# Two attentions with a gate on one Trainium2 core: parity order of the sequence, x^T phi(k) instead of v, a hand-set TensorE order, crossbar-transposed output of B

## The chip, the cores and the metric

One core of one Trainium2 chip runs the whole program. The metric is device time of one execution in microseconds (us). The kernel before was run beside every changed kernel on the same chip; its median lies between 567.8 and 569.9 us from session to session. A ratio below is the mean time of one kernel's fast runs over that of the kernel before in the same rounds, with a 95% interval, so it is not quite the ratio of the medians quoted beside it.

Names: PE is TensorE, PEld its weight loads, DVE VectorE, ACT ScalarE, POOL GpSimd, SP the engine whose queue issues most DMAs. "Matmul" without a size means 128x512 bf16 with 128 rows of contraction. Scores are q . k of B, PV is the product of the softmax weights with V, and a chunk is four heads of B. `Ob` is what PV gives, by rows; `OBT` is its transpose, which the output product needs. The crossbar is what a transposing DMA goes through. The kv stretch runs from the last matmul of v (later of x^T phi(k)) to the first of V.

## The reference, cut to what matters

```python
# x = A_x: (1, 2048, 1024) bf16; H = 32 heads of Dh = 32; wqkv: (1024, 3072); wo: (1024, 1024)
g = sigmoid((x * gate_w).sum(-1, keepdims=True))
# A: linear attention
phi = lambda t: where(t > 0, t + 1, exp(t)) + 1e-6
kv  = einsum("bhsd,bhse->bhde", phi(k), v)          # per head, 32x32, over all positions
z   = sum over s of phi(k)
a   = (phi(q) kv) / (phi(q) . z + 1e-6)  @ A_wo
# B: each position sees 8 keys, at distance 0, 2, 4, ..., 14
b   = softmax(q . k[s - 2*w] * Dh**-0.5, w = 0..7) v[s - 2*w]  @ B_wo
out = g * a + (1 - g) * b
```

Two facts carry the change. A query of B only ever sees keys of its own parity. And kv = phi(k)^T v = phi(k)^T x Wv, so it can be had as (x^T phi(k))^T Wv, without v.

## The kernel before

It keeps x^T in SBUF (`xT`, 8 blocks of 128 x 2048) and has three stages. Cuts are marked.

```python
# stage 1: k of A, v of A, kv, Wo products
nc.sync.dma_start_transpose(out=xT[:, :, 0:128], in_=x[0:128, :])
WkA = load_w("WkA", A_wqkv, D)                       # 2 MB, same queue
for s0, s1_ in ((128, 512), (512, 1024), (1024, S)):
    nc.sync.dma_start_transpose(out=xT[:, :, s0:s1_], in_=x[s0:s1_, :])
# ... pk = phi(x WkA): 256 matmuls; vA = x WvA: 256 matmuls ...
for c in range(KT):
    kvp = ps_kv.tile([P, P + 1], F32, name="kvp", tag="kv")
    for t in range(NB):
        nc.tensor.matmul(kvp[:], lhsT=pk[:, t, c * P:(c + 1) * P], rhs=vA[:, t, c, :], ...)
    # ... mask to the diagonal blocks (DVE), transpose on PE, copy (ACT) into KVT ...
# ... W2 = KVT^T WoA: 16 matmuls, copies alternating between ACT and DVE ...

# stage 2: B. 18 tiles of 113 queries (the first 127) with 128 keys each; V is projected once per tile
for c in range(KT):                                  # 4 heads at a time
    # ... kT, qT of these heads: 64 matmuls ...
    for g, tiles in enumerate(GROUPS):               # 6 groups of 3 tiles
        # 12 scores (32 rows each) -> exp on ACT -> mask on DVE -> 12 PV matmuls
        # -> reciprocal and scale on DVE -> Ob
        for tt, (q0, w, k0) in enumerate(tiles):
            nc.tensor.transpose(out=tr[:, tt, 0:w], in_=Ob[0:w, tt]..., identity=ident[0:w, 0:w])
        for w, ts in parts:
            nc.scalar.copy(out=OBT[:, c, ...], in_=tr[:, ts, 0:w])

# stage 3, for each quarter of the rows: q of A, phi, denominator, then both output products
for b in range(4):
    for c in range(KT):
        # 8 matmuls pjq -> phi -> pq
        nc.tensor.matmul(den[:], lhsT=Zb[:, c, :], rhs=pq[:], start=True, stop=True)
        # ln, exp on ACT; pqs = pq * that on DVE
    # ... 4 x 2 x (8 matmuls OBT x WoB, 8 matmuls pqs x W2), combine, store ...
```

The order on each engine is not written here: a scheduler in the kernel framework places the instructions, from the order in which the program is written and its own estimate of times.

The softmax here doesn't subtract the row's maximum and nothing guards it: scores larger than these inputs give would overflow.

## Time and profile before

| | before |
|---|---|
| time, median (lowest to highest) | 568.17 us (567.44 to 569.76), 3 runs |
| PE busy | 530.1 us, 93% |
| DVE, ACT busy | 252.7 us (44%), 232.9 us (41%) |
| matmuls of 128x512 | 2128 |

Lines of the page's first two parts for the kernel before: busy time, share and instruction count of an engine; then busy tenths of PE and the granted TensorE clock in 40 slices of the span.

```profile
...
PE 530.1 (93%) x3495; PEld 242.9 (43%) x3560; DVE 252.7 (44%) x469; ACT 232.9 (41%) x372; POOL 15.5 (3%) x62
...
PE   2999999996999999999999999969999999999997
...
PEclk9999999999799999999999999988999999999999
...
```

PE is the bound, but a busy PE is no measure of how full it is. Count instead: steady matmuls start 0.216 us apart (the skill, "TensorE: Matmul & The Clock Gate", section "Back-to-back issue gap", gives N/2.4 + 2.5 ns for an isolated matmul on a warm array; the trace agrees with that, and not with the shorter pace that the section gives for real kernels). 2128 of them are 460 us. The other 108 us are what a change can still take. PE in each stretch of the kernel before, cut at the boundaries that the chain of waits shows (stretch, its length, busy time and instructions, granted clock, DMA share, GB/s):

```profile
...
core 0: us, PE busy (x), PEclk, DMA share, GB/s
0.00:14.10 14.10, 3.57 (x8) 1.00 0.92 236
...
125.70:146.50 20.80, 13.61 (x151) 0.92 0.00 1
...
224.50:368.00 143.50, 138.61 (x1562) 1.00 0.03 9
368.00:382.30 14.30, 9.76 (x161) 0.87 0.00 1
382.30:564.90 182.60, 176.70 (x783) 0.98 0.07 23
...
```

125.7 to 146.5 holds 16 matmuls of 128x512 and 128 of 128x129: it is the kv sums and the Wo products. 224.5 to 368 is seven chunks of B's attention, 20.5 us each, of which 64 projection matmuls are 13.8. 368 to 382.3 is the last chunk, with PE busy 9.8 of 14.3 us.

A piece of one such chunk, PE instructions in order of time (start, length, line, shapes, count; in brackets idle time before and what ended it):

```profile
...
230.47 0.27 PE L243 MATMUL s_1929<-qT,kT 32*128 32x113 bf16 x6
230.81 0.32 PE L270 MATMUL tr<-ident,Ob 113*128 113x113 bf16 x3
231.06 0.28 PE L243 MATMUL s_1929<-qT,kT 32*128 32x113 bf16 x6
231.27 0.60 PE L230 MATMUL pjkq<-xT,WkB_86 128*128 128x512 bf16 x2
231.71 0.46 PE L257 MATMUL oB<-V,PT_1362 128*128 128x33 bf16 x12
232.02 0.81 PE L230 MATMUL pjkq<-xT,WkB_86 128*128 128x512 bf16 x3
...
```

The scheduler cuts the 12 scores in two and puts three transposes between (0.25 us to the start of what follows). PE is never idle for long, but 1.1 us of each group's 3.4 us is not projection (20.5 and 13.8 us over six groups).

### The profile page before, as it was taken

What the parts mean: (1) busy time and instruction counts of PE and PEld (TensorE: products, weight loads), DVE (VectorE), ACT (ScalarE), POOL (GpSimd) and SP (SyncE); (2) the same over time, 40 slices, a digit from 0 to 9 for tenths busy, and PEclk for the clock granted to TensorE, in tenths of its full rate; (3) what the DMA queues carried; (4) which work ended last, traced back from release to release, by engine and by line L of the source; (5) the groups of instructions that cost most, each with busy time, mean ns of one, the idle gap of its engine ahead of it and who ended that gap; (6) DMA issues with size and microseconds to landing.
All of it is one profiled execution on the core that took longest, in us unless ns stands there. A gap on an engine that the chain in (4) does not pass through costs nothing.

```text
span 568.5 us, 8370 instructions
## 1 busy us (share of the span) xinstructions
PE 530.1 (93%) x3495; PEld 242.9 (43%) x3560; DVE 252.7 (44%) x469; ACT 232.9 (41%) x372; POOL 15.5 (3%) x62
## 2 busy tenths in 40 slices
PE   2999999996999999999999999969999999999997
PEld 0444444444344444444444444433344344344343
DVE  1467971003311112755665575575524534533542
ACT  1233333333211112665575575565514623622631
POOL 9100000000000000000000000000000000000000
PEclk9999999999799999999999999988999999999999
DMA  9997460200202011000020000000010010010011
GB/s 236 280 349 246 119 195 4 71 1 1 74 1 74 1 30 45 2 3 1 1 75 1 2 1 2 2 2 0 19 39 17 1 56 20 0 48 28 1 37 38
DMA packets 40246, 30.17 MB, mean 53 GB/s; under 512 B 17552, under 2 KB 38032, under 8 KB 40208
## 3 DMA queue, kind: packets, MB, share of 16 engines
q1 hardware_dynamic: 40208, 29.63, 17.4%
q8 instruction: 28, 0.46, 0.3%
q14 instruction: 10, 0.08, 0.1%
HBM read 21.23 MB, written 4.19 MB: 45 GB/s over the span
## 4 chain that ended last, share of the span: by engine, by line
PE 68%; DVE 16%; ACT 8%; DMA 3%; issue 3%; SPq 1%; DVEq 0%; ACTq 0%
PE pj L129 14%; PE pjkq L230 14%; PE pjv L210 11%; PE pa L326 8%; PE pb L320 7%; DVE pq L305 3%; ACT ld L310 3%; PE pjq L298 3%; PE oB L257 3%; DVE Ob L265 2%; PE den L308 2%; PE tr L270 2%; ACT PT_1362 L249 2%; DMA xT<-in_A_x_dram 2%; DVE gjunk L153 2%
## 5 line engine op out<-in xcount | busy, mean ns | idle before, releaser
L129 PEld LDWEIGHTS <-xT 128*128 128x128 bf16 x512 | 50.6, 99 | 74.6 <-issue 9.2
L328 DVE SCALAR_TENSOR_TENSOR osb<-pa,gall,ob 128x512 bf16<-128x512 f32 x32 | 23.7, 750 | 56.7 <-PE pa L326 52.3
L323 ACT ACTIVATE ob<-pb,omgall 128x512 f32<-128x512 f32 x32 | 22.0, 687 | 60.5 <-PE pb L320 52.5
L210 PEld LDWEIGHTS <-xT 128*128 128x128 bf16 x288 | 28.5, 99 | 36.7 <-issue 2.2
L235 DVE CAST qT<-pjkq 128x512 bf16<-128x512 f32 x32 | 22.0, 688 | 42.4 <-PE pjkq L230 39.6
L129 PE MATMUL pj<-WkA_67,xT 128*128 128x512 bf16 x126 | 30.9, 407 | 10.7 <-DMA WkA_67<-in_A_wqkv_dram 8.0
L138 ACT ACTIVATE e<-pj 128x512 f32<-128x512 f32 x32 | 19.1, 597 | 51.5 <-PE pj L129 38.5
L320 PEld LDWEIGHTS <-OBT 128*128 128x128 bf16 x256 | 25.2, 98 | 29.7 <-issue 0.8
L310 ACT ACTIVATE ld<-den,eps 128x512 f32<-128x512 f32 x32 | 22.0, 687 | 35.7 <-PE den L308 35.7
L218 DVE CAST V<-pjv 128x512 bf16<-128x512 f32 x18 | 12.5, 694 | 52.3 <-PE pjv L210 52.3
L233 ACT CAST kT<-pjkq 128x512 bf16<-128x512 f32 x32 | 18.7, 586 | 37.7 <-PE pjkq L230 37.7
L320 PE MATMUL pb<-WoB_1336,OBT 128*128 128x512 bf16 x128 | 34.0, 385 | 0.0
L210 PE MATMUL pjv<-WvB_82,xT 128*128 128x512 bf16 x141 | 32.6, 392 | 1.1 <-DVE W_1311 L187 0.8
L230 PE MATMUL pjkq<-xT,WkB_88 128*128 128x512 bf16 x116 | 32.3, 380 | 0.8 <-issue 0.6
L230 PE MATMUL pjkq<-xT,WqB_695 128*128 128x512 bf16 x124 | 32.6, 379 | 0.3
L230 PE MATMUL pjkq<-xT,WkB_86 128*128 128x512 bf16 x119 | 31.8, 379 | 0.7 <-issue 0.5
L298 PE MATMUL pjq<-xT,WqA_1729 128*128 128x512 bf16 x122 | 31.3, 394 | 1.1 <-DVE qT L235 0.6
L147 ACT CAST vA<-pj 128x512 bf16<-128x512 f32 x32 | 18.8, 587 | 33.0 <-PE pj L129 31.9
L216 ACT CAST V<-pjv 128x512 bf16<-128x512 f32 x18 | 10.6, 588 | 52.9 <-PE pjv L210 50.1
L230 PE MATMUL pjkq<-xT,WqB_693 128*128 128x512 bf16 x124 | 31.8, 379 | 0.2
L320 PE MATMUL pb<-WoB_1338,OBT 128*128 128x512 bf16 x120 | 31.8, 379 | 0.2
L210 PE MATMUL pjv<-WvB_84,xT 128*128 128x512 bf16 x141 | 31.1, 379 | 0.2
(267 smaller groups left out, 771.4 us busy)
## 6 DMA issues: line engine op xcount, KB each, us to landing
xt<-in_A_x_dram SPq DMA_DIRECT2D x16, 256.0 KB, 2.6
out_dram<-osb SPq DMA_DIRECT2D x32, 128.0 KB, 1.7
WkA_67<-in_A_wqkv_dram SPq DMA_DIRECT2D x1, 1024.0 KB, 5.8
WkA_69<-in_A_wqkv_dram SPq DMA_DIRECT2D x1, 1024.0 KB, 8.2
WvA_74<-in_A_wqkv_dram SPq DMA_DIRECT2D x1, 1024.0 KB, 5.5
WvA_76<-in_A_wqkv_dram SPq DMA_DIRECT2D x1, 1024.0 KB, 7.8
WoA_78<-in_A_wo_dram SPq DMA_DIRECT2D x1, 1024.0 KB, 11.6
WoA_80<-in_A_wo_dram SPq DMA_DIRECT2D x1, 1024.0 KB, 13.3
```

What stands on the lines that cost most here:

```text
L129: nc.tensor.matmul(pj[:], lhsT=xT[:, kt, t * P:(t + 1) * P], rhs=W[half][:, kt, :], start=(kt == 0), stop=(kt == KT - 1))
L138: nc.scalar.activation(out=e[:], in_=pj[:], func=ACT.Exp)
L147: nc.scalar.copy(out=vA[:, t, half * 4:(half + 1) * 4, 0:P], in_=pj[:].rearrange("p (c e) -> p c e", c=4))
L210: nc.tensor.matmul(pj[:], lhsT=xT[:, kt, k0:k0 + P], rhs=WvB[half][:, kt, :], start=(kt == 0), stop=(kt == KT - 1))
L230: nc.tensor.matmul(pj[:], lhsT=W[c // 4][:, kt, (c % 4) * P:(c % 4 + 1) * P], rhs=xT[:, kt, cols], start=(kt == 0), stop=(kt == KT - 1))
L235: nc.vector.tensor_copy(out=dst[:, cols], in_=pj[:])
L298: nc.tensor.matmul(pj[:], lhsT=WqA[c // 4][:, kt, (c % 4) * P:(c % 4 + 1) * P], rhs=xT[:, kt, cols], start=(kt == 0), stop=(kt == KT - 1))
L310: nc.scalar.activation(out=ld[:], in_=den[:], func=ACT.Ln, bias=eps[:])
L320: nc.tensor.matmul(pb[:], lhsT=OBT[:, c, tb * P:(tb + 1) * P], rhs=WoB[half][:, c, :], start=(c == 0), stop=(c == KT - 1))
L323: nc.scalar.activation(out=ob[:], in_=pb[:], func=ACT.Copy, scale=omgall[:, tb:tb + 1])
L326: nc.tensor.matmul(pa[:], lhsT=pqs[:, c, t * P:(t + 1) * P], rhs=W2[half][:, c, :], start=(c == 0), stop=(c == KT - 1))
L328: nc.vector.scalar_tensor_tensor(out=osb[:, ncols], in0=pa[:], scalar=gall[:, tb:tb + 1], in1=ob[:], op0=ALU.mult, op1=ALU.add)
```

## The change

Its intent: fewer matmuls, no PE transposes, no stretch in which PE waits.

- **Parity order.** x is read, and the result written, even rows first, then odd. Keys of a query are then 8 neighbours, tiles are 112 queries (128 for the first of each parity), V of B is projected on 16 tiles and shifted copies are made by DMAs inside SBUF: 32 matmuls fewer.
- **x^T phi(k).** 256 matmuls in place of the 256 of v, then 64 of 128x128 with Wv in place of 128 of 128x129. z comes from 15 adds of 128x1024 on DVE and eight small fp32 products. No kv transposes.
- **Crossbar.** Ob goes to OBT by a transposing DMA. That needs 112 or 128 partitions; 113 and 127 do not fit (the skill, "DMA: Bandwidth & Descriptors", section "DMA Transpose (X-bar)", asks for a multiple of 16).
- **Order.** All of PE is under a fixed order, the order of writing. Scores and PV of chunk c are written among the projections of chunk c+1, Wo products among those of V, denominators among the output products.

The core of the diff (long; cut):

```diff
-    nc.sync.dma_start_transpose(out=xT[:, :, 0:128], in_=x[0:128, :])
-    WkA = load_w("WkA", A_wqkv, D)
-    for s0, s1_ in ((128, 512), (512, 1024), (1024, S)):
-        nc.sync.dma_start_transpose(out=xT[:, :, s0:s1_], in_=x[s0:s1_, :])
+    WkA = load_w("WkA", A_wqkv, D, eng=nc.scalar, parts=2)
+    for s0, s1_ in ((0, 128), (128, 256), (256, 512), (512, 1024), (1024, 1536), (1536, S)):
+        nc.sync.dma_start_transpose(out=xT[:, :, s0:s1_], in_=rows(x, s0, s1_))
 ...
+    with tc.manual_schedule(engines={PE}):
 ...
+            for half in range(2):
+                for kt in range(KT):
+                    pj = ps_1.tile([P, 512], F32, name="g_ps", tag="p1")
+                    for t in range(NB):
+                        nc.tensor.matmul(pj[:], lhsT=xrow[:, t, kt * P:(kt + 1) * P],
+                                         rhs=pk[:, t, half * 512:(half + 1) * 512], ...)
+                    nc.scalar.copy(out=g_[:, kt, :], in_=pj[:])
+            # zacc: 15 adds over t; gate: 16 reductions
+            for half in range(2):
+                kvp = ps_1.tile([P, 4, P], F32, name="kv_ps", tag="p1")     # one bank
+                for i in range(4):
+                    for kt in range(KT):
+                        nc.tensor.matmul(kvp[:, i, :], lhsT=WvA[half][...], rhs=G[half][...], ...)
+                    nc.vector.tensor_tensor(out=KVT[:, half * 4 + i, :], in0=kvp[:, i, :], in1=bdmask[:], ...)
 ...
-                    nc.tensor.transpose(out=tr[:, tt, 0:w], in_=Ob[0:w, tt]..., identity=ident[0:w, 0:w])
-                    nc.scalar.copy(out=OBT[:, c, ...], in_=tr[:, ts, 0:w])
+                        nc.sync.dma_start_transpose(
+                            out=OBT[:, c, q0:q0 + m * w].rearrange("p (t s) -> p t s", t=m),
+                            in_=Ob[0:w, t0:t0 + m].rearrange("p t i e -> p (t i e)"))
 ...
+                for g in range(len(GROUPS)):          # 5 groups, of 4, 4, 4, 3, 3 tiles
+                    ev.append((3 + 12.8 * g, lambda g=g: scores(g)))
+                    ev.append((3 + 12.8 * g + 17, lambda g=g: pv(g)))
 ...
+                interleave(list(kq_units(c, kqt)), [e for e in ev if e[0] < 64])   # ev: chunk c-1
```

## The prediction

> **What bounds it now.** TensorE. The page's first part gives PE 530.1 of 568.5 us (93%); VectorE is at 44%, ScalarE at 41%. The chain of waits shows eight 128x512 matmuls in 1.73 us, 0.216 us each; the Trainium skill, "TensorE: Matmul & The Clock Gate", section "Back-to-back issue gap", states N/2.4 + 2.5 ns, so the trace agrees and these matmuls cannot be made faster, only fewer or closer together. There are 2128 of them: 460 us. The other 108 us, by stretches of the chain:
> - 0 to 14.1: steady work starts only when the second transposed piece of x has landed; only 8 matmuls before it. About 12.4 us lost.
> - 125.7 to 146.5: kv sums, transposes and the product with Wo, PE waiting on VectorE and ScalarE; granted clock 0.78 at the end. 16 useful big matmuls in 20.8 us: about 17 lost.
> - 224.7 to 368: seven periods of 20.5 us, of which 64 projections are 13.8; the rest is scores, PV, transposes (three take about 0.26 us, six groups a period) and turns between them.
> - 368 to 382.3: the last chunk's attention with little to fill it, PE busy 9.8 of 14.3.
> - 382.3 to 564.9: four blocks of 45.65 us holding 200 big matmuls (43.3).
>
> **What the change does.** Big matmuls 2128 -> 2096 (V on 16 tiles, not 18): -7 us. V projection of A (256) becomes x^T phi(k) (256): equal. 128 kv matmuls of 129 columns become 64 of 128; the 8+144 TensorE transposes go; Wo products move into the V stage. Attention goes among the next chunk's projections in a fixed order, and its tail among the query projection of A. 128/112-row tiles suit the crossbar: the skill, "DMA: Bandwidth & Descriptors", section "DMA Transpose (X-bar)", wants a multiple of 16 partitions; no run yet shows a transfer that breaks this. Before, a crossbar transpose held the queue 0.17 us per 128x128 block (20.3 us for 120); 18 blocks in 8 transfers a period are then some 3 us plus fixed cost, off the critical path.
>
> Added VectorE work in the first stage: 16 adds of 128x1024 for z (estimate 1.2 us each from the 1.22 us gate reduction), which the order puts, with 10 gate reductions, among the 32 phi(k) (1.12 us each). That is about 62 us against 55.4 of TensorE, and the first reduction waits for x rows queued behind all transposes (about 26 us). Six PSUM banks absorb most; I expect a PE stall of about 5 us there.
>
> **Sum (us).** Start 9; k projection 55.4 + stall 5; x^T phi(k) 55.5; kv and z 7.5; V with Wo products 59; first k/q chunk 14; seven periods of 19.0 = 133 (13.8 + scores 2.7 + PV 1.9 + turns and small stalls; no transposes); query block with last attention 20.5; remaining 736 big matmuls 159.5 + 2; end 3.5. Total 524.
>
> **Prediction: 524 us, 512 to 538.** Faster by over 2%: 0.97; within 2%: 0.025; slower: 0.005.
>
> **What would show each step.** PE busy about 97%; steady matmuls from 9 us or less; idle PE before k-projection matmuls released by VectorE phi(k), some 5 us in total between 25 and 70 us; about 7 us between the last x^T phi(k) and first V matmul, clock near 1; a period of 18.5 to 19.5 us; PE idle under 1 us in the query block; output blocks without waits on pq or ld.
>
> **What would make it wrong.** SBUF-to-SBUF transposes slower than those from HBM: then Ob (two buffers) holds VectorE, and PV and projections follow (period over 20). Two projection banks with in-order ScalarE and VectorE (VectorE some 14.5 us of each 19) stalling PE. Fp32 z matmuls costing more than 0.3 us each. VectorE not holding up the first stage (then 518).

## The result

| | before, same rounds | after |
|---|---|---|
| time, median (lowest to highest) | 567.81 us (567.31 to 569.76) | 518.45 us (516.1 to 519.9), 4 runs |
| ratio | | 0.9121 (0.908 to 0.9162) |
| PE busy | 530.1 us, 93% | 494.4 us, 96% |
| DVE busy | 252.7 us | 262.6 us |
| ACT busy | 232.9 us | 209.4 us |

The same lines of the page for the changed kernel:

```profile
...
PE 494.4 (96%) x3328; PEld 230.2 (45%) x3328; DVE 262.6 (51%) x553; ACT 209.4 (40%) x323; POOL 8.1 (2%) x27
...
PE   2899999999899999999999999989999999999996
...
PEclk9899999999999999999999999999999999999999
...
```

PE by stretch in the changed kernel, cut at its own stages (first matmuls, k projection, x^T phi(k), kv and z, V with Wo products, first k/q chunk, seven chunks with attention, query block with the last attention, the rest, the end):

```profile
...
core 0: us, PE busy (x), PEclk, DMA share, GB/s
0.00:15.40 15.40, 3.41 (x8) 1.00 0.94 201
15.40:72.75 57.35, 56.34 (x249) 0.97 0.88 262
72.75:128.00 55.25, 55.25 (x260) 1.00 0.06 20
128.00:136.56 8.56, 6.27 (x82) 1.00 0.42 137
136.56:195.29 58.73, 58.73 (x274) 1.00 0.32 94
195.29:209.70 14.41, 14.41 (x72) 1.00 0.52 168
209.70:333.90 124.20, 123.13 (x1445) 1.00 0.22 47
333.90:354.40 20.50, 18.00 (x219) 1.00 0.15 28
354.40:513.50 159.10, 158.84 (x736) 1.00 0.08 27
...
```

256 matmuls of x^T phi(k) take 55.25 us, 0.2158 us each: nothing is left there. The last stage, from 354.4, holds 736 big matmuls in 159.1 us, again 0.216 each; in the kernel before each quarter there lost some 2.4 us (45.65 us for 200 matmuls). The gain by stage: kv 20.8 to 8.6 us, with 3.5 us of Wo products moved; a chunk 20.5 to 17.6; the end of attention and stage 3 together 196.9 (from 368 to 564.9) to 179.6 (from 333.9 to 513.5).

PE in one chunk of the changed kernel, in order of time, to be laid beside the same view of before:

```profile
...
227.30 1.25 PE L266 MATMUL kq_ps<-xT,WkB_101 128*128 128x512 bf16 x5
228.39 0.46 PE L315 MATMUL oB<-V,PT_1008 128*128 128x33 bf16 x12
228.69 1.89 PE L266 MATMUL kq_ps<-xT,WqB_568 128*128 128x512 bf16 x8
230.51 0.38 PE L292 MATMUL s_1826<-kqt 32*128 32x112 bf16 x16
230.82 1.04 PE L266 MATMUL kq_ps<-xT,WkB_101 128*128 128x512 bf16 x4
...
```

Sixteen scores of 32 rows go in 0.31 us, 16 PV matmuls in 0.41 us (12 in 0.30), uncut, and no transposes: 12.8 projections fit between two groups.

One thing went backwards. PE's first lines:

```profile
...
9.55 3.41 PE L153 MATMUL pk_ps<-WkA_72,xT 128*128 128x512 bf16 x8 [9.55 <-DMA xT<-in_A_x_dram]
15.44 20.85 PE L153 MATMUL pk_ps<-WkA_72,xT 128*128 128x512 bf16 x88 [2.47 <-DMA xT<-in_A_x_dram]
36.70 1.89 PE L153 MATMUL pk_ps<-WkA_72,xT 128*128 128x512 bf16 x8 [0.41 <-DVE pk L140]
38.78 1.89 PE L153 MATMUL pk_ps<-WkA_72,xT 128*128 128x512 bf16 x8 [0.19 <-DVE pk L140]
...
```

Steady matmuls start at 15.4 us, later than before (14.1), and not at 9 as predicted. The lines of 36.7 and 38.8 are the stall behind DVE that was forecast at 5 us; it is 0.8 us in all, in three waits. Another 1.9 us went in the 88 matmuls before it: they took 20.9 us, at a granted clock of 0.92.

### The profile page after: what moved, and what is told of

Read it like the earlier page. It is cut to its first block, busy times and chain, and to the rows that moved or that the text cites. A ratio compares the mean times of both kernels' runs of the same rounds, so it can differ in the third digit from the quotient of the medians.

```text
span 517.1 us, 8148 instructions
## 1 busy us (share of the span) xinstructions
PE 494.4 (96%) x3328; PEld 230.2 (45%) x3328; DVE 262.6 (51%) x553; ACT 209.4 (40%) x323; POOL 8.1 (2%) x27
## 4 chain that ended last, share of the span: by engine, by line
PE 82%; DVE 9%; SPq 5%; DMA 3%; issue 1%; ACT 0%; DVEq 0%
PE d_ps L410 21%; PE kq_ps L266 21%; PE v_ps L237 11%; PE g_ps L165 11%; PE d_ps L362 8%; SPq L96 5%; PE oB L315 3%; DVE pk L140 2%; DVE gjunk L179 2%; DMA OBT<-Ob 2%; DVE e L139 1%; PE q_ps L362 1%; PE den L395 1%; DMA xrow<-in_A_x_dram 1%; PE pk_ps L153 1%; PE kv_ps L191 1%
## 5 line engine op out<-in xcount | busy, mean ns | idle before, releaser
L165 PE MATMUL g_ps<-pk,xrow 128*128 128x512 bf16 x256 | 55.4, 379 | 0.0
L153 PEld LDWEIGHTS <-xT 128*128 128x128 bf16 x256 | 25.6, 101 | 46.7 <-DMA xT<-in_A_x_dram 12.7
L153 PE MATMUL pk_ps<-WkA_72,xT 128*128 128x512 bf16 x128 | 31.7, 409 | 12.8 <-DMA xT<-in_A_x_dram 12.0
L139 DVE TENSOR_SCALAR e<-e 128x512 f32<-128x512 f32 x64 | 26.6, 421 | 32.1 <-ACT e L138 32.1
L165 PEld LDWEIGHTS <-xrow 128*128 128x128 bf16 x256 | 25.0, 98 | 30.2
L237 PEld LDWEIGHTS <-xT 128*128 128x128 bf16 x256 | 25.1, 98 | 30.0
L324 DVE TENSOR_TENSOR Ob<-oB,rd 128x256 bf16<-128x256 f32 x80 | 31.4, 393 | 3.8 <-DMA OBT<-Ob 2.6
L266 PE MATMUL kq_ps<-xT,WkB_103 128*128 128x512 bf16 x128 | 32.9, 380 | 0.0
L266 PE MATMUL kq_ps<-xT,WqB_570 128*128 128x512 bf16 x128 | 32.9, 379 | 0.0
L266 PE MATMUL kq_ps<-xT,WkB_101 128*128 128x512 bf16 x128 | 32.3, 379 | 0.0
L266 PE MATMUL kq_ps<-xT,WqB_568 128*128 128x512 bf16 x128 | 32.2, 379 | 0.0
L410 PE MATMUL d_ps<-WoA_93,pqs 128*128 128x512 bf16 x128 | 31.7, 379 | 0.0
L410 PE MATMUL d_ps<-WoB_3861,OBT 128*128 128x512 bf16 x128 | 31.2, 379 | 0.0
L410 PE MATMUL d_ps<-WoB_3859,OBT 128*128 128x512 bf16 x128 | 30.7, 379 | 0.0
L410 PE MATMUL d_ps<-WoA_95,pqs 128*128 128x512 bf16 x128 | 30.7, 379 | 0.0
L237 PE MATMUL v_ps<-WvB_99,xT 128*128 128x512 bf16 x128 | 30.6, 379 | 0.0
## 6 DMA issues: line engine op xcount, KB each, us to landing
WvA_89<-in_A_wqkv_dram SPq DMA_DIRECT2D x1, 1024.0 KB, 15.4
```

What stands on the lines that cost most here:

```text
L139: nc.vector.tensor_scalar(out=e[:], in0=e[:], scalar1=1.0, scalar2=1e-6, op0=ALU.min, op1=ALU.add)
L153: nc.tensor.matmul(pj[:], lhsT=xT[:, kt, t * P:(t + 1) * P], rhs=WkA[half][:, kt, :], start=(kt == 0), stop=(kt == KT - 1))
L165: nc.tensor.matmul(pj[:], lhsT=xrow[:, t, kt * P:(kt + 1) * P], rhs=pk[:, t, half * 512:(half + 1) * 512], start=(t == 0), stop=(t == NB - 1))
L237: nc.tensor.matmul(st["pj"][:], lhsT=xT[:, kt, t * P:(t + 1) * P], rhs=WvB[half][:, kt, :], start=(kt == 0), stop=(kt == KT - 1))
L266: nc.tensor.matmul(st["pj"][:], lhsT=W[c // 4][:, kt, (c % 4) * P:(c % 4 + 1) * P], rhs=xT[:, kt, cols], start=(kt == 0), stop=(kt == KT - 1))
L324: nc.vector.tensor_tensor(out=Ob[:, 2 * b:2 * b + m], in0=oBv[:, b, 0:m, :, 0:Dh], in1=rd[:, b, 0:m].broadcast_to([P, m, 4, Dh]), op=ALU.mult)
```

## The experiments

Twelve runs, in three sessions: 1 to 4 on one chip, 6 to 9 on one, and 5 with 10 to 12 on one.

**1. Is it the hand-set order?** The changed kernel without it:

```diff
-    with tc.manual_schedule(engines={PE}):
+    with ExitStack():
```

> The changed kernel, written in the same interleaved order, but the TensorE order is left to the scheduler. Theory A (the hand-set order is what gains in the attention stage): 535 us or more, the period of a chunk back near 20 us. Theory B (the order in which the program is written already carries most of it, the scheduler keeps it): 516 to 526 us, period 17.6 to 18.5 us. I lean to B.

Measured: 512.91 us (512.6 to 513.36), ratio 0.9004 (0.898 to 0.9028). Faster than the changed kernel; neither theory had that. Theory A falls: a chunk takes 17.6 us here too. The order that gains is the one in which the program is written, and the scheduler keeps it. Where the fixed order loses, the trace shows. PE in the kv stretch, first the changed kernel:

```profile
...
127.84 0.61 PE L191 MATMUL kv_ps<-G_572,WvA_89 128*128 128x128 bf16 x8
128.83 0.61 PE L191 MATMUL kv_ps<-G_572,WvA_89 128*128 128x128 bf16 x8 [0.38 <-DVE KVT L194]
129.82 0.61 PE L191 MATMUL kv_ps<-G_572,WvA_89 128*128 128x128 bf16 x8 [0.38 <-DVE KVT L194]
...
```

and the same stretch under the scheduler:

```profile
...
127.67 4.02 PE L191 MATMUL kv_ps<-G,WvA 128*128 128x128 bf16 x64
131.53 1.90 PE L198 MATMUL z_ps<-ones,zacc 128*128 128x1 f32 x16
...
```

The four groups of `kv_ps` share one PSUM bank, and the framework lets PE write to a bank only after DVE has read what stands in it (the skill, "PSUM — Partial Sum Buffer", section "PSUM bank collisions raise a hardware error", says that two engines on one bank at once are an error; no run here made one, they show only the wait). In the fixed order PE stands 0.38 us at each of six groups. Under the scheduler DVE reads one group every 0.44 to 0.55 us while PE goes on with the next without a wait. So neighbouring groups must lie in different banks, which means that the scheduler takes the two halves in turn; the trace doesn't name the banks. (Run 9, which keeps the fixed order and only moves the reads, loses the wait too.) From the first kv matmul to the first of V the scheduler's kernel takes 5.6 us in place of 8.6. The rest of its 6 us (of the two spans, 517.1 and 511.1) is at a late crossbar transfer (below) and at the last PV, where the fixed order lets PE stand 1.2 us behind Ob while matmuls of the next block are ready.

**2. Is it the interleaved writing?** Attention written after its own chunk's projections, as before, order left to the scheduler:

```diff
             for c in range(KT):
                 kqt = kq.tile([P, 2, S], BF16, name="kqt", tag="kq")
-                ev = carry + (attention_events(c - 1, prev) if c else [])
-                interleave(list(kq_units(c, kqt)), [e for e in ev if e[0] < 64])
-                carry = [(p - 64, f) for p, f in ev if p >= 64]
+                interleave(list(kq_units(c, kqt)), [])
+                for p_, f in sorted(attention_events(c, kqt), key=lambda e: e[0]):
+                    f()
 ... (and the same at the query projection: nothing is interleaved there)
```

> The changed kernel with attention written after its own chunk's projections as in the kernel before, and TensorE order left to the scheduler. If order and interleaving are what gains, the period returns to the 20.5 us of before less about 1.6 us of TensorE transposes, some 19 us, and the last attention shows again as a stretch with PE idle (about 4 us): 532 to 542 us. Rival (the gain of the stage comes from having no transposes and fewer, larger groups): 522 us or less.

Measured: 525.24 us (524.9 to 526.7), ratio 0.9228 (0.9196 to 0.9261). The period is 19.0 us as expected (two periods in 38.1, the next two in 37.7), but the total fell between the two theories, since it was set against 518 us, while the fair partner is run 1 with 512.9. Against that, writing attention among the next projections is worth 12.3 us. Nearly all of it falls before the query block: both kernels start their first k/q matmul at 192.0 us, and the last one starts at 340.3 us here, at 328.7 in run 1. That is some 1.3 to 1.4 us in each of seven periods, and one wait of 1.8 us at 224.8. The last attention costs next to nothing: PE is idle there for 1.3 us in four waits, not the 4 us expected, since the scheduler fills it with the query projection.

**3. What does any interleaving hide?** The same writing, PE held to it:

> Attention written after its own chunk and TensorE held to exactly that order, so nothing fills the wait for exponentials. Scores wait for one set of four banks: about 2.5 us for each of five groups plus a tail, some 11 us of extra time in each of eight chunks: 590 to 620 us, with PE idle before scores released by ScalarE. If it is under 560 the wait behind the exponentials is not what interleaving hides.

Measured: 610.13 us (609.73 to 611.1), ratio 1.0712 (1.0682 to 1.0743): the time is in the range, the account of it only in part. The edit is that of run 2 with the fixed order kept. From the page's costliest groups (busy time and mean ns; idle time of PE before them and what ended it):

```profile
...
L315 PE MATMUL oB<-V,PT 128*128 128x33 bf16 x576 | 24.4, 192 | 37.3 <-DVE Ob L324 37.2
L292 PE MATMUL s<-kqt 32*128 32x112 bf16 (+1 forms) x576 | 18.2, 252 | 29.9 <-ACT PT L301 29.9
...
```

The wait behind the exponentials is there, 29.9 us of idle PE before scores. But PE waits longer, 37.2 us, before PV, until DVE has read the one set of PV banks; that was not foreseen. PE's busy time is longer than the changed kernel's as well, 517.6 against 494.4 us: the granted clock is 0.902 over the run, the lowest of all, and 0.74 from 209 to 400 us. A fixed order is only as good as what is written.

**4. TensorE transposes in place of the crossbar.** Order otherwise kept; the transposes go into the unused part of the PV banks, since the other banks are taken:

```diff
-                        nc.sync.dma_start_transpose(out=OBT[:, c, ...], in_=Ob[0:w, t0:t0 + m]...)
+                    trv = st["oB"][:, :, 264:392].bitcast(BF16)
+                    # 8 units after PV: nc.tensor.transpose(out=trv[...], in_=Ob[0:w, tt]...), then ScalarE copies to OBT
```

> The changed kernel with 144 TensorE transposes and ScalarE copies in place of the crossbar transfers; order otherwise kept, the transposes 8 units after PV, in the free part of the PV banks. Theory (transposes cost PE time): about 85 ns each plus turns, 1.6 us a chunk, 13 us in all, and up to 10 more where PV waits for the shared banks: 530 to 542 us. Rival (they would hide, the crossbar saves nothing on PE): 521 us or less. If the two stalls behind late crossbar transfers in the trace (1.3 us at 275, 1.2 us at 354) matter, those vanish here.

Measured: 550.27 us (546.82 to 552.93), ratio 0.9656 (0.9606 to 0.9705): 32 us worse, more than the theory allowed. A chunk takes 21.1 us in place of 17.6. PE in this kernel, in order of time:

```profile
...
225.19 0.37 PE L336 MATMUL oB<-ident,Ob 112*128 112x112 bf16 x4 [0.49 <-DVE Ob L327]
225.40 0.38 PE L269 MATMUL kq_ps<-xT,WkB 128*128 128x512 bf16 x1
...
237.42 0.37 PE L336 MATMUL oB<-ident,Ob 128*128 128x128 bf16 x4 [0.38 <-DVE Ob L327]
237.62 0.38 PE L269 MATMUL kq_ps<-xT,WqB 128*128 128x512 bf16 x1
...
```

Four transposes themselves are 0.2 to 0.3 us, so 1.0 to 1.4 us a chunk, 8 to 11 us in all. Much of the rest is waiting: 16.1 us of idle PE in the table of waits stand before transposes, released by DVE's Ob. Of the 30.4 us between the two spans (547.5 and 517.1), PE is busy for 11.2 more and idle for 19.2 more. The two waits behind late crossbar transfers are gone, as they must be.

**5. Is that waiting the fixed order's?** The same with the scheduler's order (the edit of run 1):

> TensorE transposes as in the run before, but TensorE order left to the scheduler. That run was 32 us slower than the changed kernel, and 16 us of it were PE idle before PV, held by the fixed order. Theory: what remains here is the work of 144 transposes and their turns, 12 to 16 us over the scheduler-ordered kernel: 525 to 530 us. If it stays at 540 or more, the waits come from the shared PV banks, not from the order.

Measured: 538.98 us (538.77 to 539.41), ratio 0.948 (0.9462 to 0.9498). A miss, and just short of the 540 that was to convict the banks. (The 16 us that the expectation puts before PV stood before the transposes.) The period is still 21.1 us. Two periods, in the columns of the table of stretches above:

```profile
...
213.90:235.10 21.20, 19.99 (x230) 1.00 0.01 2
235.11:256.18 21.07, 19.73 (x224) 1.00 0.00 1
...
```

Idle PE before transposes shrinks to 5.3 us in all, yet a chunk is no shorter. Beside run 1, whose chunk has PE busy 17.3 of 17.6 us, it is 3.5 us longer: PE is busy for 2.5 us of that and idle for 1.0. So under the scheduler most of the loss is time that PE's own instructions take, transposes and the scores and projections that they cut apart, though short waits also hide in it, since a matmul's recorded time is longer than its step (0.38 against 0.216 us). Of the 25.9 us between the spans of runs 1 and 5 (511.1 and 537.0), PE is busy for 18.2 and idle for 7.7; some records are missing from both traces, so this split is rough. The 11 us between runs 4 and 5 are in the kv stretch and at the last attention, not in the chunks.

So the crossbar is worth 26 to 32 us against these transposes. Why they cost so much more than their own 8 to 11 us stays open: the shared PV banks, the extra ScalarE copies and the cut order were not told apart, and transposes with a bank of their own were not run.

**6. The start.**

```diff
-    WkA = load_w("WkA", A_wqkv, D, eng=nc.scalar, parts=2)
-    for s0, s1_ in ((0, 128), (128, 256), (256, 512), (512, 1024), (1024, 1536), (1536, S)):
-        nc.sync.dma_start_transpose(out=xT[:, :, s0:s1_], in_=rows(x, s0, s1_))
+    load_x((0, 128))                                   # all on the one queue
+    WkA0 = load_w("WkA", A_wqkv, D, parts=2, which=(0,))
+    load_x((128, 256), (256, 512), (512, 1024))
+    WkA1 = load_w("WkA", A_wqkv, D, parts=2, which=(1,))
+    load_x((1024, 1536), (1536, S))
```

> Only the order of the first loads: first piece of x, first half of the k weights, x to row 1024, second half of the weights, rest of x, all on one queue. Theory (the 2 MB of weights issued at once from a second queue starve the transposes of x, so that steady matmuls start at 15.4 us): first matmul at about 7.5 us and no gap of over 2 us after it, 6 us less in all: 510 to 514 us. Rival (the crossbar transposes of strided rows are slow by themselves): start stays at 14 us or later, 517 us or more.

Measured: 511.99 us (510.4 to 515.34), ratio 0.8989 (0.8962 to 0.9016), against 0.9133 for the changed kernel. PE's first lines:

```profile
...
7.25 5.14 PE L160 MATMUL pk_ps<-WkA,xT 128*128 128x512 bf16 x16 [7.25 <-DMA WkA<-in_A_wqkv_dram]
12.80 10.84 PE L160 MATMUL pk_ps<-WkA,xT 128*128 128x512 bf16 x48 [0.40 <-DMA xT<-in_A_x_dram]
24.83 1.47 PE L160 MATMUL pk_ps<-WkA,xT 128*128 128x512 bf16 x6 [1.20 <-DMA xT<-in_A_x_dram]
```

The theory's numbers hold: first matmul at 7.25 us, no gap above 1.2 us, and the rival falls, since the first strided rows now land in 3.4 us. But the edit changes the queue of the weights as well as the order, so it doesn't show which of the two counts. The first 128 rows of x landed 3.2 us after issue in the kernel before, where nothing was ahead of them; in the changed kernel 2 MB of weights were issued at the same moment from ScalarE's queue, and those rows came at 9.55 us.

**7. V on 18 tiles**, straight into place (no copies in SBUF):

```diff
-                nc.tensor.matmul(..., lhsT=xT[:, kt, t * P:(t + 1) * P], rhs=WvB[half][:, kt, :], ...)   # t < 16
+                nc.tensor.matmul(..., lhsT=xT[:, kt, QT[t][2]:QT[t][2] + P], rhs=WvB[half][:, kt, :], ...)   # t < 18
```

> V of B projected at the 18 tile offsets straight into its place, as before, instead of 16 tiles and moves in SBUF: 32 more matmuls of 128x512 at 0.216 us. Theory: V stage 58.7 to 65.6 us, total plus 7: 524 to 527 us. Rival (the moves and their waits cost about what they save): 520 us or less.

Measured: 528.93 us (526.98 to 529.56), ratio 0.9266 (0.9241 to 0.9291): 8 us more than the changed kernel by the ratios (the medians, from two sessions, differ by 10.5), and a little above the range that was expected. With the moves gone, the copies of V also alternate between ScalarE and DVE. The V stage takes 68.6 us in place of 58.7: 6.9 us for 32 matmuls, two waits of 0.6 and 0.7 us for a projection bank, and a slower clock at its start in this profile (20 matmuls in 5.7 us, granted clock 0.76). The moves inside SBUF cost nothing that shows.

**8. x^T phi(k) alone**, in the kernel before (the first half of the diff above, PE order by the scheduler, its own two banks for kv):

> The kernel before with x^T phi(k) in place of v alone. Theory: kv stretch from 13.3 to about 8 us, no kv transposes; the Wo products still stand apart, so of the 12 us that this stretch lost between the kernels about 5 to 6 come from the algebra: 560 to 564 us. Rival (the algebra alone carries it): 556 us or less. If the z adds hold VectorE up there it is 566 or more.

Measured: 563.04 us (562.86 to 563.78), ratio 0.9881 (0.9857 to 0.9906), so less than 2% but clear of noise. From the last x^T phi(k) to the first V matmul it takes 14.6 us in place of 20.8, so the algebra gives 6.2 us. The changed kernel's 8.6 us there come from moving the Wo products among V as well; as they still cost 3.5 us, the move itself saves some 2.5.

**9. Mending three things in the fixed order.** Run 6 with

```diff
                                          start=(kt == 0), stop=(kt == KT - 1))
+                for i in range(4):
                     nc.vector.tensor_tensor(out=KVT[:, half * 4 + i, :], ...
-            WoB = load_w("WoB", B_wo, 0)
+            WoB = load_w("WoB", B_wo, 0, eng=nc.gpsimd)
```

> The changed kernel with the one-queue start, the kv masking moved behind the four matmul groups that share its bank (six waits of 0.38 us in the trace), and the output weights of B loaded through the POOL queue, so the crossbar transfers do not stand behind 2 MB in theirs (one stall of 1.3 us). Expected: 6 + 2.3 + 1.3 us less than the changed kernel, 507 to 511 us. If only the start counts, the same as the start alone.

Measured: 510.29 us (509.81 to 512.5), ratio 0.896 (0.8937 to 0.8983). In the range, but one of its three reasons failed, and the total alone does not tell it from run 6, whose interval of the ratio overlaps. The kv stretch went from 8.56 to 5.3 us by the trace. The weights through POOL did not help: the longest crossbar transfer took 9.2 us from issue to landing (8.4 in the changed kernel; the median is 2.4 in both), and PE's wait for Ob rose from 2.2 to 3.3 us.

**10. The weights after the last transfer.** Run 9 with the load on SP, behind a one-element copy from the last piece of OBT into the weight tile, so that it must wait:

```diff
+            if gate is not None:
+                nc.vector.tensor_copy(out=w[0:1, 0, 0:1], in_=gate)
-            WoB = load_w("WoB", B_wo, 0, eng=nc.gpsimd)
+            WoB = load_w("WoB", B_wo, 0, gate=OBT[0:1, KT - 1, S - 1:S])
```

> Hand-set order, one-queue start, kv masks moved, and the output weights of B loaded only after the last crossbar transfer has landed (by a one-element copy that the load must follow). Theory (2 MB of weights in the DMA engines delay the crossbar transfers to 8 to 9 us and so hold Ob, VectorE and PV): the longest transfer falls to 3 us or less, the stall of 1.1 to 2.1 us between 245 and 275 us is gone, total 506.5 to 509 us. Rival (the slow transfer has another cause): it stays, 510 us or more.

Measured: 508.0 us (507.48 to 508.19), ratio 0.8932 (0.8915 to 0.895). The stall between 245 and 275 us is gone (one wait for Ob is left, 1.2 us at the last PV), and the longest transfer takes 4.1 us (not under 3). From issue to landing over all 64 transfers, first the changed kernel, then this one:

```profile
...
DMA to landing us min/median/max: 2.2/2.4/8.4
```

```profile
...
DMA to landing us min/median/max: 2.2/2.3/4.1
```

So 2 MB of ordinary loads delay the crossbar transfers, from SP's queue (8.4 us) as from POOL's (9.2), and two buffers of Ob do not carry PE over such a delay in the fixed order. By time alone runs 9 and 10 are not clearly apart (their intervals overlap); the traces carry this.

**11. The changed kernel again**, beside the next run:

> The changed kernel unaltered, on the chip of the runs beside it, since the scheduler-ordered one beat it across two sessions only. If that was real, its ratio to the kernel before stays at 0.910 to 0.914, about 1.2% above the 0.900 of the scheduler's order; if it was the session, it comes out at 0.903 or less.

Measured: 519.5 us (518.11 to 519.98), ratio 0.9133 (0.9112 to 0.9153). Run 1's lead was real.

**12. The mends with the scheduler's order:** run 6, the kv edit of run 9 and the edit of run 1.

> One-queue start, kv masks behind their four matmul groups, and TensorE order left to the scheduler with the interleaved writing kept. Theory (the gains are in different stages and add): scheduler order 0.900 less 6.5 us of start (0.011): ratio 0.888 to 0.892, 506 to 508 us. If the earlier start is eaten by VectorE, which then has the gate and z work sooner in its way, 510 us or more.

Measured: 507.43 us (507.06 to 508.43), ratio 0.8927 (0.8908 to 0.8946). The time is as expected, the ratio just outside. It beats both kernels, and is level with run 10: once the waits are mended, the fixed order and the scheduler's are equal. Its longest crossbar transfer is 8.5 us, so the late load of run 10 could still be added; that was not run.

## Why the prediction was right

It said 524 us, 512 to 538; 518.45 was measured. The sum against the stretches of the trace after:

| step | predicted | measured | |
|---|---|---|---|
| start | 9 | 15.4 | too low by 6.4 |
| k projection with stall | 60.4 | 57.35 | 248 of the 256, as 8 fall in the start; stall 0.8, not 5; 1.9 to a lower clock |
| x^T phi(k) | 55.5 | 55.25 | right |
| kv and z | 7.5 | 8.6 | six bank waits not seen |
| V with Wo products | 59 | 58.7 | right |
| first k/q chunk | 14 | 14.4 | right |
| seven periods | 133 (19.0 each) | 124.2 (17.6 each, one with a stall of 1.3) | too high by 8.8 |
| query block, last attention | 20.5 | 20.5 | right, but idle PE 2.5, not under 1 |
| 736 matmuls | 161.5 | 159.1 | no waits at all |
| end | 3.5 | 3.6 | right |

The main idea held: matmuls at 0.216 us are the floor, and the change takes away turns, transposes and gaps between them. PE busy came to 96% (97 foretold), the clock to 0.997, and the output blocks show no waits on pq or ld. Three terms were off, and partly cancelled: the start was 6.4 us too low, the first stage 3.1 and the periods 8.8 too high. That the total lies within 6 us owes something to luck.

- **"Start 9".** The recorded text gives no reason for the 9; I had counted bytes and issue times, and took it that x would come first because it is needed first. Issued together, weights and transposes share the DMA engines (the skill, "DMA: Bandwidth & Descriptors", section "Issuing engines are not separate DMA queues", says just that: they interleave, whichever engine starts them; the trace agrees, 9.55 us against 3.96 for the first rows). Run 6, which changes only the order and the queue of these loads, removes the delay; which of the two it takes was not told apart.
- **"Stall 5".** The mechanism was right: the gate reduction waits for rows of x (until 33.3 us) and DVE lags. Its work was over-counted, in two ways. Only 11 of the 15 adds for z ran before the last phi(k), where the prediction put all of them. And DVE instructions overlap. Some of them in a row, in the changed kernel:

```profile
...
34.48 0.42 DVE L139 TENSOR_SCALAR e<-e 128x512 f32<-128x512 f32 x1
34.82 1.22 DVE L179 CUSTOM_DVE_ANT_0 gjunk<-xrow,gw_row 128x1024 bf16<-128x1024 bf16 x1
...
35.96 0.68 DVE L140 SCALAR_TENSOR_TENSOR pk<-pk_ps,e 128x512 bf16<-128x512 f32 x1
36.56 0.41 DVE L139 TENSOR_SCALAR e<-e 128x512 f32<-128x512 f32 x1
...
```

  An operation listed with 0.42 us is followed 0.34 us later, one with 1.22 us 1.14 us later. I added durations; starts are what add up. The 26 phi(k) still to do and the work between them took 48 us from 33.3 on, where my durations give 55, and the six banks carried that. How much each of the two took off the stall was not tested. The skill, "Perfetto Trace Analysis", section "Optimizing Scalar/DVE Operations", says that the end of one instruction overlaps the next; the trace agrees with about 0.08 us.
- **"Scores 2.7".** I took 12 scores from groups that the scheduler had cut in two. Uncut, 5 groups take 3 x 0.31 + 2 x 0.26 = 1.45 us a chunk. The difference, 1.25 us in each of seven periods, is the 8.8 by which the periods were too high. With PV at 1.85 and 64 projections at 13.8 this is 17.1 of the 17.6 measured.

What the prediction did not ask is which part of the change carries the gain. The runs answer: of a ratio of 0.9121, run 8 gives 0.012 to x^T phi(k) alone, run 7 about 0.014 to the 16 tiles, runs 1 and 2 about 0.022 to the interleaved writing, runs 4 and 5 some 0.05 to the crossbar against transposes in the PV banks; these parts lean on each other and do not add exactly. The fixed PE order as such costs 6 to 7 us (spans 517.1 and 511.1, ratios 0.9133 and 0.9004), and the start as written about 8 us (ratio 0.9133 to 0.8989).

## What to carry to other kernels

Write independent work where a wait will fall, and then try whether the scheduler keeps it before nailing the order down; a fixed order also fixes every wait that you did not foresee, and two small ones (a shared PSUM bank, a late DMA) ate some 4 us here. Issue first what has to land first, with the bulk behind it: weights issued at the same moment from a second queue came with the first rows of x 5.6 us later, and a bulk load beside crossbar transfers delayed them from either queue that was tried. When you add up an engine's work from a trace, add start-to-start times of a busy stretch, not durations.

## What the Trainium skill lacked or had wrong

- "TensorE: Matmul & The Clock Gate", section "Back-to-back issue gap": it gives about 131 ns as the sustained pace of N=512 in real kernels. Here 256 in a row take 55.25 us, 216 ns each; the formula that it calls that of an isolated matmul is the right one here.
- The same page, Part 1, gives a floor of about 25 ns from start to start. PV matmuls of 33 columns show it (12 in 0.30 us, 25 ns), but scores of 32 rows and 112 columns, in four row groups in turn, go 16 in 0.31 us, 19 ns each. So the floor is not one for matmuls on different row groups, which the page treats in a part of its own.
- The same page, Part 4, gives 275 to 390 ns for a 128x128 TensorE transpose. In run 4 the trace records 211 ns for one (median of 144), and four in a row start what follows after 0.21 us, 53 ns each.
- "VectorE: DVE Perf Modes", section "The three transpose paths", sets 390 ns on TensorE against 1309 ns on the crossbar, and the rules of that page advise TensorE if a PSUM destination is OK. They lack the case in which every bank is in use: here the crossbar (queue held 1.19 us, landing after 2.4 us, both medians) won by 26 to 32 us over transposes into shared banks.
- "DMA: Bandwidth & Descriptors": no page says how far ordinary loads delay a crossbar transfer in flight. Here the longest took 8.4 us beside 2 MB (9.2 when the load came through POOL) and 4.1 us when the load came after all of them; the median is 2.3 to 2.4 in each case.
- The same page says that starting DMAs on several engines saves only the time to start them. It does not warn of a loss: here, with the weights on a second queue, the first 128 rows of x came at 9.55 us, against 3.96 in the kernel before, with one queue and these rows first.
